# The next pair's high halves and query diagonal made a third of a step earlier, and its row maxima with them

## The chip, the cores and the metric

One core of one Trainium2 chip runs the kernel. The metric is device time in microseconds (us) of one execution; lower is better. A profiled execution has a span, from the first instruction of the program to the last, and its own device time, which is a little longer.

## What is computed

```python
def _attn_ref(q, k, v):                      # 4 batches, 8 heads, 1152 positions, 64 per head
    q_pool = q.reshape(B, H, S // 2, 2, D).mean(axis=3)
    scores = scale * np.matmul(q_pool, k.transpose(0, 1, 3, 2))
    scores = scores - np.max(scores, axis=-1, keepdims=True)
    attn = np.exp(scores)
    attn = attn / (np.sum(attn, axis=-1, keepdims=True) + 1e-09)
    return np.matmul(attn, v)
...
x = attn_out as 2304 tokens of 512
x = (silu(x @ w_gate) * (x @ w_val)) @ w_out          # inner width 1536
logits = x @ phi                                      # soft mixture, 8 experts x 4 slots
slot_input = softmax(logits over tokens).T @ x
slot_out[e] = relu(slot_input[e] @ w1[e]) @ w2[e]
return softmax(logits over slots) @ slot_out
```

Queries are pooled in twos, so a head has 576 query rows against 1152 keys. Scores are worked out in the precision of float32: each operand is split into a 16-bit high half and a 16-bit low half, and the products of the halves are summed.

## The kernel before

The sixteen pairs of heads (4 batches, 4 pairs each) are worked off in sixteen steps; `steps[i]` is pair i, and step i is the attention of pair i. Step i consists of 21 units of scores (`unit`): two matmuls each (L447 and L448) into a bank of PSUM, an exponential on ScalarE (L453, tile P) that takes the row maximum off by way of a row of QH, a subtraction on GpSimd that makes the low half of the result (L460, tile PL), and three units later the products with the values (L483 to L493, tile pv). `attn` yields 42 times in a step, twice a unit; f is the share of them that is past.

Before pair i can be worked off, its operands must be made (`split_pair`) and its row maxima must be known (`row_max`).

- `load_pair` brings keys, queries and values (kr, qr, vr) from memory; the buffers for kr and qr exist once.
- `split_pair(steps[i + 1])` runs at the start of step i (step 0: after 5 yields). It adds the two pooled queries in place (L257, VectorE), casts the keys' high half kh and the queries' high half qh (ScalarE, `cast`, L211), takes the low halves ql (L271, VectorE) and kl (L273, GpSimd), copies qh into the diagonal QD (two copies, L278, VectorE), starts twelve DMAs on SyncE's queue that lay the halves out per head in KK, QQ, KL and QH, and splits the values. kh, qh and QD exist once.
- QD holds head 0's queries in the upper 64 partitions and head 1's in the lower 64, with zeros elsewhere, so that one matmul against kh gives scores of both heads.
- `row_max` works the maxima from high halves alone: 18 matmuls of 512 columns and 9 of 128 (L366, tile mx, two banks), 21 reductions on VectorE (L372, L381, tile mp), one last reduction (L384, tile nm); two yields later ScalarE scales it (L352, tile mt) and starts a DMA from its own queue (L390) that writes the row of QH. The pair stands in `has_max` from then on. L448 is the matmul that reads this row.
- `maxima(n)` advances a single stream of all pairs' maxima to its n-th piece: 21 pieces for pair 0, 22 for each later pair. In step i (from 1 on) the main loop advances the pieces of pair i + 1 evenly between two shares of the step, `MX_BEG` and `MX_END`. In step 0 two other constants do it for pair 1.

From step 2 to step 8 the weights of the second stage are converted beside the attention (tiles r, lo, wgv, w2p); from step 4 on, matmuls of the second stage (L724 to L729, tiles g and v) fill in, paced by the steps (`MOE_PACE`): one block of 256 tokens until step 8 and 5.1 more until the end of step 15. The rest of the second stage and the mixture follow.

The order of each engine's instructions is laid down when the program is built, by a planner with a modelled timeline; what is written first goes first where both are ready, units of scores and the end of an accumulation are lifted by 20 places, and `after` and `not_before` set single orders by hand (a cast of the keys behind the mt DMA of the maxima before, the QD copies behind the nm before them). Each engine then works strictly in that order.

Of the kernel before, what the change touches and what calls it, by code (L numbers as in the profile page):

```python
# [10 lines left out]
F16 = mybir.dt.float16  # L11
# [26 lines left out]
ST_STEPS, ST_OF = 1, 3  # L38
HP_U0, HP_U1 = 20, 20
MX0, MXP = 21, 22  # L40
MX_BEG, MX_END = 0.05, 0.72
MX0_END, MX1_BEG, MX1_END = 0.34, 0.34, 0.84
PREP_LEAD = 3
HP_F = 20
# [33 lines left out]
def tile_pool_attention_glu_softmoe(  # L78
# [13 lines left out]
    nc = tc.nc  # L92
    B, NP, _, S = kT.shape
    SQ = qT.shape[4]
    D = 64
    P = 128
    NCH = S // P
# [4 lines left out]
    E, _, FE = w1.shape  # L102
# [24 lines left out]
    def after(ins, name):  # L127
        dep = mybir.DependencyInfo(mybir.DependencyClass.NoSync, mybir.DependencyReason.SCHED_ONLY)
        tc.add_manual_dep(ins.ins, name, dep, reason="pace")

    def not_before(ins, lead):

        if len(marks) > lead >= 0:
            after(ins, marks[-1 - lead])
# [31 lines left out]
    at = attn_stack.enter_context(tc.tile_pool(name="attn", bufs=1, side="right"))  # L166
# [14 lines left out]
    steps = [(b, p) for b in range(B) for p in range(NP)]  # L181
    raw = {}
    last_max = [None]
    QHs = {}
    st = {}

    NKQ = 2
    KLs = [at.tile([D + 1, 2, S], F16, name=f"KL{i}") for i in range(NKQ)]
    for t in KLs:
        nc.vector.memset(t[D:D + 1, :, :], 16.0)  # L190

    QD = at.tile([P, 2, SQ], F16, name="QD")
# [15 lines left out]
    def cast(what, b, p, dst, src):  # L208

        if b * NP + p < CAST_STEPS and what in CASTS:  # L210
            ins = nc.scalar.copy(dst, src)  # L211
        else:
            ins = nc.vector.tensor_copy(out=dst, in_=src)
        if p == 1 and b == 0 and what in "kvq":
            not_before(ins, 0)
        return ins

    def sub(what, b, p):

        i = b * NP + p  # L220
        return nc.gpsimd if i < len(SUBS) and what in SUBS[i] else nc.vector
# [6 lines left out]

    def first_split(kd, qd, KK, KL, QQ, QH):

        q = qd[:, :SQ]
        nc.vector.tensor_tensor(out=q, in0=q, in1=qd[:, SQ:], op=ALU.add)
        nc.vector.tensor_copy(out=QQ[:D, :], in_=q)
        nc.vector.tensor_copy(out=KK[:D, :], in_=kd)
        nc.scalar.copy(KK[D:, :], kd)
        nc.scalar.copy(QH[:D, :], QQ[:D, :])
        nc.gpsimd.tensor_tensor(out=QQ[D:, :], in0=q, in1=QQ[:D, :], op=ALU.subtract)
        nc.gpsimd.tensor_tensor(out=KL[:D, :], in0=kd, in1=KK[:D, :], op=ALU.subtract)

    def split_pair(b, p, first=None):  # L240
        kr, qr, vr = raw.pop((b, p))
        i = (b * NP + p) % NKQ
        KL = KLs[i]
        VV = at.tile([P, 2, NCH, 2, D + 1], F16, tag="VV", bufs=2, name=f"VV{b}_{p}")
        KK = at.tile([P, 2, S], F16, tag="KK", bufs=2, name=f"KK{b}_{p}")
        QQ = at.tile([P, 2, SQ], F16, tag="QQ", bufs=2, name=f"QQ{b}_{p}")
        QH = at.tile([D + 1, 2, SQ], F16, tag="QH", bufs=2, name=f"QH{b}_{p}")
        QHs[b, p] = QH
        for hd in range(2):
            st[b, p, hd] = (KK[:, hd, :], KL[:, hd, :], QQ[:, hd, :], QH[:, hd, :], VV[:, hd], vr[:, hd])  # L250
        if first:
            first_split(*first, KK[:, 0, :], KL[:, 0, :], QQ[:, 0, :], QH[:, 0, :])
            maxima(9)

        r = slice(D if first else 0, P)
        qp = qr[r, 0, :]
        add = sub("a", b, p).tensor_tensor(out=qp, in0=qp, in1=qr[r, 1, :], op=ALU.add)  # L257

        if (b, p) == steps[1]:
            after(add, last_max[0])  # L260
        elif not first:
            not_before(add, ADD_LEAD)
        kh = at.tile([P, S], F16, tag="kh", bufs=1, name=f"kh{b}_{p}")
        KHs[b, p] = kh
        k_cast = cast("k", b, p, kh[r], kr[r])
        if mt_name:
            after(k_cast, mt_name[-1])
        qh = at.tile([P, SQ], F16, tag="qh", bufs=1, name=f"qh{b}_{p}")
        q_cast = cast("q", b, p, qh[r], qp).ins.name
        ql = at.tile([P, SQ], F16, tag="ql", bufs=1, name=f"ql{b}_{p}")  # L270
        q_low = sub("l", b, p).tensor_tensor(out=ql[r], in0=qp, in1=qh[r], op=ALU.subtract).ins.name  # L271
        kl = at.tile([P, S], F16, tag="kl", bufs=1, name=f"kl{b}_{p}")
        k_low = nc.gpsimd.tensor_tensor(out=kl[r], in0=kr[r], in1=kh[r], op=ALU.subtract)  # L273
        rows = [slice(0, D), slice(D, P)]
        heads = range(1 if first else 0, 2)
        if not first:
            for hd in heads:
                ins = nc.vector.tensor_copy(out=QD[rows[hd], hd, :], in_=qh[rows[hd], :])  # L278
                if nm_name:
                    after(ins, nm_name[-1])  # L280
        for hd in heads:
            nc.sync.dma_start(out=KK[:D, hd, :], in_=kh[rows[hd], :])
            nc.sync.dma_start(out=KK[D:, hd, :], in_=kh[rows[hd], :])
        for hd in heads:
            nc.sync.dma_start(out=QQ[:D, hd, :], in_=qh[rows[hd], :])
            nc.sync.dma_start(out=QQ[D:, hd, :], in_=ql[rows[hd], :])
        for hd in heads:
            nc.sync.dma_start(out=KL[:D, hd, :], in_=kl[rows[hd], :])
            nc.sync.dma_start(out=QH[:D, hd, :], in_=qh[rows[hd], :])
        v_cast = cast("v", b, p, VV[:, :, :, 0, :], vr)  # L290
        if first:
            after(k_low, q_low)
            after(v_cast, q_cast)
        nc.gpsimd.tensor_tensor(out=VV[:, :, :, 1, :D], in0=vr[:, :, :, :D], in1=VV[:, :, :, 0, :D], op=ALU.subtract)  # L294
    def row_max_first(hd):
# [59 lines left out]
    mt_name, nm_name = [], []  # L355
    has_max = {steps[0]}
# [43 lines left out]
    def later(n, fn):  # L400

        due.append((now[0] + n, fn))
# [18 lines left out]
    def maxima(n):  # L421
        while n_rm[0] < min(n, MX0 + MXP * (len(steps) - 1)):
            next(maxs)
            n_rm[0] += 1
# [38 lines left out]
    def pv_rem(acc, PH, PL, b, p, parts):  # L463

        for i in range(0, len(parts), 2):
            c = parts[i][1]
            todo = []
            for z in range(2):
                dst = acc[z * D:(z + 1) * D, 4, :]
                VV, vr = st[b, p, z][4:]  # L470
                q = slice((i + z) * REM, (i + z + 1) * REM)
                if PL is None:
                    todo.append([(dst, PH[:, q], vr[:, c, :])])
                else:
                    todo.append([
                        (dst[:, :D + 1], PH[:, q], VV[:, c, 0, :]),
                        (dst[:, :D], PH[:, q], VV[:, c, 1, :D]),
                        (dst[:, :D + 1], PL[:, q], VV[:, c, 0, :]),
# [501 lines left out]
    first = first_load()  # L980
# [52 lines left out]
    def moe_due(t):  # L1033
        for (t0, m0), (t1, m1) in zip(MOE_PACE, MOE_PACE[1:]):
            if t < t1:
                return QPB * (m0 + (m1 - m0) * (t - t0) / (t1 - t0))
        return QPB * MOE_PACE[-1][1]

    n_done = 0
    for i, (b, p) in enumerate(steps):  # L1040
        for u, _ in enumerate(attn(b, p)):
            if i == 0 and u == PHI_U:
                nc.sync.dma_start(out=ph, in_=phi.rearrange("p (d s) -> p d s", d=ND))
            tick()
            f = (u + 1) / UNITS
            if u == (SPLIT0 if i == 0 else 0):
                if i + 1 < len(steps):
                    split_pair(*steps[i + 1])
                if i + 2 < len(steps):
                    later(0 if i == 0 else LOAD_LAG, lambda k=i + 2: load_pair(*steps[k]))  # L1050

            if i:
                maxima(MX0 + MXP * i + int(MXP * min(1.0, max(0.0, f - MX_BEG) / (MX_END - MX_BEG))))
            else:
                maxima(9 + int((MX0 - 9) * min(1.0, f / MX0_END)) + int(MXP * min(1.0, max(0.0, f - MX1_BEG) / (MX1_END - MX1_BEG))))
            while i >= MOE_START and n_done < moe_due(i + f):
                if not next(moe_work, False):
                    break
                n_done += 1
            while prep and n_prep - len(prep) < (i + f - PREP_BEG) * n_prep / (PREP_END - PREP_BEG):  # L1060
                prep.pop(0)()
            if not prep and u == LOAD_U and LOAD_STEP <= i < LOAD_STEP + NEE:
                load(i - LOAD_STEP, marks[-1])
# [28 lines left out]
    for z in range(2):  # L1092
        (nc.vector.tensor_copy, nc.scalar.copy)[z](
            out=GT.rearrange("p (f h c) s -> p f h c s", h=2, c=2)[:, :, z],
            in_=t.rearrange("p (f c) h s -> p f c h s", c=2)[:, :, :, z],
# [51 lines left out]
    for e in range(4):  # L1147
        r = slice(e * NS, e * NS + E // 4 * SPE)
# [6 lines left out]
    for g in range(E // NQ):  # L1155
        for h in range(2):
# [13 lines left out]
            for e in range(NQ):  # L1170
                a = NQ * g + e
                nc.vector.tensor_copy(
                    out=hT[:, NQ * h:NQ * (h + 1), a, g, :],
                    in_=t[:, :, e * NS + SPE * a:e * NS + SPE * (a + 1)],
# [112 lines left out]
```

## Time and profile before

| | |
|---|---|
| median of 3 runs | 879.44 us (874.75, 879.44, 883.06) |
| the profiled execution's own time | 874.95 us |
| its span | 873.2 us |
| mean granted TensorE clock | 0.979 |
| busy: TensorE matmuls, weight loads | 817.1 us (94%), 579.0 us (66%) |
| busy: VectorE, ScalarE, GpSimd | 540.4 us (62%), 393.3 us (45%), 414.4 us (47%) |

PE is TensorE, PEld its weight loads, DVE VectorE, ACT ScalarE, POOL GpSimd, SP SyncE; a q behind a name is the engine's sequencer, which issues DMAs. Matmuls overlap in the array and their ends are modelled, so a stretch in which PE is called busy isn't always one in which it could take no more. The rows of a timeline give start, duration, engine, line and tiles, and in brackets how long the engine had been idle before and what ended that. The rows of windows give a stretch, its length, the busy time (and count) of PE, PEld, DVE, ACT and POOL, the granted clock as a share of 2.4 GHz, the DMA share and GB/s.

### The profile page before, as it was taken

What the parts mean: (1) busy time and instruction counts of PE and PEld (TensorE: products, weight loads), DVE (VectorE), ACT (ScalarE), POOL (GpSimd) and SP (SyncE); (2) the same over time, 40 slices, a digit from 0 to 9 for tenths busy, and PEclk for the clock granted to TensorE, in tenths of its full rate; (3) what the DMA queues carried; (4) which work ended last, traced back from release to release, by engine and by line L of the source; (5) the groups of instructions that cost most, each with busy time, mean ns of one, the idle gap of its engine ahead of it and who ended that gap; (6) DMA issues with size and microseconds to landing.
All of it is one profiled execution on the core that took longest, in us unless ns stands there. A gap on an engine that the chain in (4) does not pass through costs nothing.

```text
span 873.2 us, 23665 instructions
## 1 busy us (share of the span) xinstructions
PE 817.1 (94%) x9952; PEld 579.0 (66%) x9952; DVE 540.4 (62%) x1060; ACT 393.3 (45%) x739; POOL 414.4 (47%) x380
## 2 busy tenths in 40 slices
PE   5978988999799899999999999999999999998896
PEld 2545656776576667777777777777777777776345
DVE  7957868588777767566666666576734344445223
ACT  4545868676677743435343444335334312112112
POOL 7978666454558654646565555546445200000100
PEclk9989989999899999999999999999999999999998
DMA  6563766859577551527343453413112399358999
GB/s 196 144 157 95 228 162 229 263 135 266 137 202 194 170 135 33 135 59 141 113 108 80 127 135 102 106 31 74 26 38 38 90 304 308 61 155 222 295 284 290
DMA packets 151868, 132.48 MB, mean 152 GB/s; under 512 B 83152, under 2 KB 120720, under 8 KB 151760
## 3 DMA queue, kind: packets, MB, share of 16 engines
q1 hardware_dynamic: 149600, 130.92, 56.2%
q8 instruction: 78, 1.28, 0.6%
q10 hardware_dynamic: 2160, 0.04, 0.1%
q14 instruction: 30, 0.25, 0.1%
HBM read 84.10 MB, written 7.86 MB: 105 GB/s over the span
## 4 chain that ended last, share of the span: by engine, by line
PE 75%; DVE 12%; DMA 5%; ACT 3%; issue 2%; SPq 1%; POOL 1%; ACTq 0%; DVEq 0%
PE st L448 7%; PE st L447 7%; PE mx L366 6%; PE g L724 5%; PE g L729 5%; PE g L728 5%; PE v L724 5%; PE v L729 5%; PE v L728 5%; DVE mp L372 3%; PE pv L491 3%; PE pv L492 3%; PE pv L493 3%; PE pv L483 2%; PE hp L1160 2%
## 5 line engine op out<-in xcount | busy, mean ns | idle before, releaser
L460 POOL TENSOR_TENSOR PL<-P 128x512 f16<-128x512 f32 (+1 forms) x311 | 326.2, 1061 | 238.0 <-ACT P L453 232.0
L453 ACT ACTIVATE P<-st 128x512 f32<-128x512 f32 (+1 forms) x336 | 191.2, 582 | 215.8 <-PE st L448 182.0
L372 DVE TENSOR_REDUCE mp<-mx 128x1 f32<-128x512 f32 x270 | 180.1, 686 | 68.8 <-PE mx L366 66.2
L448 PE MATMUL st<-QH,KL 65*128 65x512 f16 (+1 forms) x576 | 145.9, 294 | 8.1 <-DMA QH<-mt 5.5
L447 PE MATMUL st<-QQ,KK 128*128 128x512 f16 (+1 forms) x576 | 146.0, 292 | 3.8 <-ACT P L453 3.6
L492 PE MATMUL pv<-VV,P 128*128 128x64 f16 x1088 | 139.8, 196 | 0.3 <-POOL VV L294 0.3
L491 PE MATMUL pv<-VV,P 128*128 128x65 f16 x1088 | 138.6, 194 | 0.9 <-DVE x L523 0.8
L493 PE MATMUL pv<-VV,PL 128*128 128x65 f16 x1088 | 135.9, 193 | 0.2 <-POOL PL L460 0.2
L724 PE MATMUL g<-xT,wgv 128*128 128x256 f16 x432 | 119.2, 276 | 3.9 <-DVE hs L736 2.7
L729 PE MATMUL g<-xT,wgv 128*128 128x256 f16 x432 | 119.1, 276 | 1.4 <-DVE wgv L689 1.4
L728 PE MATMUL g<-xT,wgv 128*128 128x256 f16 x432 | 119.0, 275 | 0.0
L491 PEld LDWEIGHTS <-P 128*128 128x128 bf16 x1088 | 104.2, 98 | 21.7 <-issue 4.1
L724 PE MATMUL v<-xT,wgv 128*128 128x256 f16 x432 | 117.9, 273 | 0.5 <-DVE wgv L689 0.5
L729 PE MATMUL v<-xT,wgv 128*128 128x256 f16 x432 | 117.9, 273 | 0.0
L728 PE MATMUL v<-xT,wgv 128*128 128x256 f16 x432 | 117.9, 273 | 0.0
L366 PE MATMUL mx<-kh,QD 128*128 128x512 f16 x270 | 105.1, 407 | 12.6 <-DVE QD L278 6.0
L493 PEld LDWEIGHTS <-PL 128*128 128x128 f16 x1088 | 104.1, 100 | 10.7 <-POOL PL L460 2.1
L492 PEld LDWEIGHTS <-P 128*128 128x128 bf16 x1088 | 103.6, 98 | 10.7 <-issue 2.3
L728 PEld LDWEIGHTS <-wgv 128*128 128x128 f16 x864 | 84.9, 98 | 21.3 <-issue 6.2
L724 PEld LDWEIGHTS <-wgv 128*128 128x128 f16 x864 | 85.3, 99 | 19.5 <-issue 3.5
L729 PEld LDWEIGHTS <-wgv 128*128 128x128 f16 x864 | 84.8, 98 | 17.6 <-DVE wgv L689 1.5
L448 PEld LDWEIGHTS <-KL 65*128 65x128 f16 x576 | 51.8, 98 | 33.5 <-issue 13.3
(184 smaller groups left out, 1190.8 us busy)
## 6 DMA issues: line engine op xcount, KB each, us to landing
w<-in_w SPq DMA_DIRECT2D x16, 1024.0 KB, 7.4
w<-in_w SPq DMA_DIRECT2D x64, 256.0 KB, 5.4
vr<-in_vP SPq DMA_DIRECT2D x16, 585.0 KB, 5.8
KK<-kh SPq DMA_DIRECT2D x62, 144.0 KB, 3.6
qr<-in_qT SPq DMA_DIRECT2D x15, 576.0 KB, 4.5
kr<-in_kT SPq DMA_DIRECT2D x15, 576.0 KB, 4.8
r<-in_w_out SPq DMA_DIRECT2D x12, 512.0 KB, 4.4
r<-in_w_gate SPq DMA_DIRECT2D x24, 256.0 KB, 5.9
```

The lines of the kernel that those rows point to most:

```text
L366: nc.tensor.matmul(t, q, kh[:, k0:k0 + kw], start=True, stop=True)
L372: nc.vector.reduce_max(out=mp[:, g, c:c + 1], in_=t, axis=AX.X)
L447: nc.tensor.matmul(t[:, o:o + w], KK[:, k], QQ[:, q0:q0 + w], start=True, stop=False)
L448: nc.tensor.matmul(t[:, o:o + w], KL[:, k], QH[:, q0:q0 + w], start=False, stop=True)
L453: marks.append(nc.scalar.activation(P32[:, :o], t[:, :o], AF.Exp, scale=1.0 / 16.0).ins.name)
L460: eng.tensor_tensor(out=PL[:, :o], in0=P32[:, :o], in1=PH[:, :o], op=ALU.subtract)
L491: nc.tensor.matmul(dst[:, :D + 1], PH[:, q], VV[:, c, 0, :], start=first, stop=False, skip_group_check=True)
L492: nc.tensor.matmul(dst[:, :D], PH[:, q], VV[:, c, 1, :D], start=False, stop=False, skip_group_check=True)
L493: nc.tensor.matmul(dst[:, :D + 1], PL[:, q], VV[:, c, 0, :], start=False, stop=(c == NCH - 1), skip_group_check=True)
L724: mm = nc.tensor.matmul(o, w[:, 0, d, f], xh, start=(d == 0), stop=False)
L728: nc.tensor.matmul(o, w[:, 0, d, f], xl, start=False, stop=False)
L729: nc.tensor.matmul(o, w[:, 1, d, f], xh, start=False, stop=(d == ND - 1))
```

## The change

The pooled add, both casts to high halves and the two QD copies leave `split_pair` for a function of their own, `split_high`. For a pair k of 2 or later it is called as soon as the maxima of pair k - 1 are complete (`has_max`) and pair k has been loaded, which is in step k - 2; `split_pair(k)` at the start of step k - 1 makes the rest as before. The maxima of pair k run from 0.9 of step k - 2 to 0.6 of step k - 1, where they ran from 0.05 to 0.72 of step k - 1. Pairs 0 and 1 keep their places. Nothing is computed more or less.

```diff
-MX_BEG, MX_END = 0.05, 0.72
+MX_BEG, MX_END = -0.1, 0.6
...
+    highs = {}
+
+    def split_high(b, p, first=None):
+        kr, qr, _ = raw[b, p]
...
+        add = sub("a", b, p).tensor_tensor(out=qp, in0=qp, in1=qr[r, 1, :], op=ALU.add)
...
+        kh = at.tile([P, S], F16, tag="kh", bufs=1, name=f"kh{b}_{p}")
+        KHs[b, p] = kh
+        k_cast = cast("k", b, p, kh[r], kr[r])
+        if mt_name:
+            after(k_cast, mt_name[-1])
+        qh = at.tile([P, SQ], F16, tag="qh", bufs=1, name=f"qh{b}_{p}")
+        q_cast = cast("q", b, p, qh[r], qp).ins.name
+        rows = [slice(0, D), slice(D, P)]
+        for hd in range(0 if first else 2):
+            ins = nc.vector.tensor_copy(out=QD[rows[hd], hd, :], in_=qh[rows[hd], :])
+            if nm_name:
+                after(ins, nm_name[-1])
+        highs[b, p] = r, qp, kh, qh, q_cast
+
     def split_pair(b, p, first=None):
-        kr, qr, vr = raw.pop((b, p))
+        if not first and (b, p) not in highs:
+            split_high(b, p)
+        kr, qr, vr = raw[b, p]
...
+        if first:
+            split_high(b, p, first)
+        del raw[b, p]
+        r, qp, kh, qh, q_cast = highs.pop((b, p))
...
-            if i:
-                maxima(MX0 + MXP * i + int(MXP * min(1.0, max(0.0, f - MX_BEG) / (MX_END - MX_BEG))))
-            else:
+            if i == 0:
                 maxima(9 + int((MX0 - 9) * min(1.0, f / MX0_END)) + int(MXP * min(1.0, max(0.0, f - MX1_BEG) / (MX1_END - MX1_BEG))))
+            for k in (i + 1, i + 2):
+                if 2 <= k < len(steps):
+                    if steps[k - 1] in has_max and steps[k] in raw and steps[k] not in highs:
+                        split_high(*steps[k])
+                    if steps[k] in highs or steps[k] in QHs:
+                        part = (i + f - (k - 1) - MX_BEG) / (MX_END - MX_BEG)
+                        maxima(MX0 + MXP * (k - 1) + int(MXP * min(1.0, max(0.0, part))))
```

## Rows read from the trace of the kernel before

**Rows 1.** The page's head and busy time of the engines.
```profile
span 873.2 us, 23665 instructions
...
PE 817.1 (94%) x9952; PEld 579.0 (66%) x9952; DVE 540.4 (62%) x1060; ACT 393.3 (45%) x739; POOL 414.4 (47%) x380
```
**Rows 2.** Windows: steps 1 to 7, then steps 8 to 14.
```profile
43.70:296.90 253.20, 227.35 (x3005) 157.49 (x3005) 189.47 (x351) 170.90 (x325) 163.57 (x140) 0.95 0.68 189
296.90:646.00 349.10, 345.37 (x4284) 253.00 (x4284) 226.18 (x434) 146.56 (x274) 188.88 (x163) 1.00 0.40 93
```
**Rows 3.** Waits of PE from 40 to 300 us: total, times, longest.
```profile
PE mx L366 <- DVE QD L278: 6.0, 2, 3.2
PE st L448 <- DMA QH<-mt: 5.5, 3, 3.8
...
PE st L448 <- DMA KK<-kh: 2.6, 1, 2.6
PE mx L366 <- ACT kh L211: 2.2, 1, 2.2
```
**Rows 4.** Timeline of PE where one pair hands over to the next.
```profile
77.71 0.38 PE L448 MATMUL st<-QH,KL 65*128 65x512 f16 x1 [0.79 <-DMA QH<-mt]
...
82.48 1.06 PE L366 MATMUL mx<-kh,QD 128*128 128x512 f16 x2 [3.22 <-DVE QD L278]
...
114.30 1.07 PE L366 MATMUL mx<-kh,QD 128*128 128x512 f16 x2 [2.75 <-DVE QD L278]
...
230.10 1.01 PE L448 MATMUL st<-QH,KL 65*128 65x512 f16 x2 [3.85 <-DMA QH<-mt]
```
**Rows 5.** Windows: stretches at half clock behind those places; the sum takes all four.
```profile
82.50:85.90 3.40, 3.40 (x20) 1.68 (x21) 1.93 (x3) 0.60 (x1) 1.82 (x2) 0.50 0.47 126
113.20:120.00 6.80, 5.70 (x42) 2.72 (x43) 4.61 (x7) 1.94 (x4) 3.55 (x4) 0.50 0.74 199
...
sum 20.40, PE 18.14 PEld 9.39 DVE 11.51 ACT 5.45 POOL 11.17; mean PE 4.53 PEld 2.35 DVE 2.88 ACT 1.36 POOL 2.79
```
**Rows 6.** Timelines of DVE, ACT and POOL from 72.5 to 83 us.
```profile
73.89 0.18 DVE L384 TENSOR_REDUCE nm<-mp 128x9 f32<-128x27 f32 x1
...
79.11 3.31 DVE L278 COPY QD<-qh 64x576 f16<-64x576 f16 x2
...
76.02 1.14 ACT L211 CAST kh<-kr 128x1152 f16<-128x1152 f32 x1
77.06 0.67 ACT L211 CAST qh<-qr 128x576 f16<-128x576 f32 x1
...
78.53 2.88 POOL L273 TENSOR_TENSOR kl<-kr,kh 128x1152 f16<-128x1152 f32 x1
```
**Rows 7.** Groups by line, 43.7 to 296.9 us: busy, mean ns, idle before.
```profile
L453 ACT ACTIVATE P<-st 128x512 f32<-128x512 f32 (+1 forms) x148 | 83.8, 583 | 43.8 <-PE st L448 26.3 <-PE pv L492 9.8 <-POOL PL L460 2.6
...
L278 DVE COPY QD<-qh 64x576 f16<-64x576 f16 x14 | 12.0, 860 | 0.1
...
L211 ACT CAST kh<-kr 128x1152 f16<-128x1152 f32 x7 | 8.1, 1152 | 1.6 <-DMA QH<-qh 1.1 <-ACT mt L352 0.6
...
L211 ACT CAST qh<-qr 128x576 f16<-128x576 f32 x7 | 4.8, 680 | 0.0
```
**Rows 8.** All QD copies of the run: shortest, median, longest ns.
```profile
L278 DVE COPY QD<-qh x30: 289/694/2459, 24.9 to 594.2; 64x576 f16<-64x576 f16 x30
```
**Rows 9.** Waits of ACT from 43.7 to 296.9 us, and one mt issue.
```profile
ACT mt L352 <- DVE nm L384: 3.1, 1, 3.1
...
225.18 0.48 ACTq L390 DMA_DIRECT2D QH<-mt  x1
```
**Rows 10.** Chain that ended last: the load of kr for pair 5, and mt.
```profile
128.28 0.58 SPq L201
...
144.93 3.14 DMA QH<-mt
```
**Rows 11.** DMA issues of the page: count, KB, median us to landing.
```profile
kr<-in_kT SPq DMA_DIRECT2D x15, 576.0 KB, 4.8
```

More of the change, by code (lines that the diff above doesn't have):

```diff
@@ L238, in first_split @@
         nc.gpsimd.tensor_tensor(out=KL[:D, :], in0=kd, in1=KK[:D, :], op=ALU.subtract)
-    def split_pair(b, p, first=None):
-        kr, qr, vr = raw.pop((b, p))
[L242 to L253, printed above, removed]
+    highs = {}
+    def split_high(b, p, first=None):
+        kr, qr, _ = raw[b, p]
         r = slice(D if first else 0, P)
@@ L269, in split_pair @@
         q_cast = cast("q", b, p, qh[r], qp).ins.name
+        rows = [slice(0, D), slice(D, P)]
[4 more added lines that the diff above has]
+        highs[b, p] = r, qp, kh, qh, q_cast
+    def split_pair(b, p, first=None):
+        if not first and (b, p) not in highs:
+            split_high(b, p)
+        kr, qr, vr = raw[b, p]
+        i = (b * NP + p) % NKQ
+        KL = KLs[i]
+        VV = at.tile([P, 2, NCH, 2, D + 1], F16, tag="VV", bufs=2, name=f"VV{b}_{p}")
+        KK = at.tile([P, 2, S], F16, tag="KK", bufs=2, name=f"KK{b}_{p}")
+        QQ = at.tile([P, 2, SQ], F16, tag="QQ", bufs=2, name=f"QQ{b}_{p}")
+        QH = at.tile([D + 1, 2, SQ], F16, tag="QH", bufs=2, name=f"QH{b}_{p}")
+        QHs[b, p] = QH
+        for hd in range(2):
+            st[b, p, hd] = (KK[:, hd, :], KL[:, hd, :], QQ[:, hd, :], QH[:, hd, :], VV[:, hd], vr[:, hd])
+        if first:
+            first_split(*first, KK[:, 0, :], KL[:, 0, :], QQ[:, 0, :], QH[:, 0, :])
+            maxima(9)
+        if first:
+            split_high(b, p, first)
+        del raw[b, p]
+        r, qp, kh, qh, q_cast = highs.pop((b, p))
         ql = at.tile([P, SQ], F16, tag="ql", bufs=1, name=f"ql{b}_{p}")
@@ L275, in split_pair @@
         heads = range(1 if first else 0, 2)
[L276 to L280, printed above, removed]
         for hd in heads:
```

## The prediction

> **What bounds the kernel now.** I read the page's head first: the matmuls are called busy for 817.1 of 873.2 us [rows 1], so TensorE sets the time and a change like this one, which computes nothing less, can win only time in which TensorE stands idle or runs slowly. Then windows, to see where that is. I cut the run at the first score matmul of pair 1 and of pair 8. In steps 1 to 7 TensorE is busy 227.35 of 253.2 us, which leaves 25.9 us idle, 36.2 us a step; in steps 8 to 14 it is busy 345.37 of 349.1 us, which leaves 3.7 us [rows 2]. The late steps are filled by the second stage's matmuls; whatever the change does for order there is worth next to nothing. So the case is decided in the early steps, where no other engine is full either: VectorE 189.47, ScalarE 170.9 and GpSimd 163.57 of 253.2 us [rows 2].
>
> Third, the waits of TensorE there. The long ones all hang on the two things that the change moves: 6.0 us for the diagonal QD, 5.5 us for the row of QH that the maxima's DMA brings, and 2.6 and 2.2 us in the hand-over from step 0 to step 1 [rows 3]. The timeline shows them at the hand-overs: 0.79 and 3.22 us where pair 2 begins, 2.75 us where pair 3 begins, 3.85 us where pair 6 begins [rows 4]; the third wait for QH is what is left of the 5.5, 0.9 us. Fourth, the clock. Behind these places stand stretches with a granted clock of 0.50, the 1.2 GHz level, 20.4 us in the sum, with TensorE busy for 18.14 us of it [rows 5]; before each of them it had stood idle for one of these waits. A matmul at half clock takes twice its time, so 18.14 / 2 = 9.1 us of them are the clock's.
>
> **The maxima end earlier.** The maxima of pair k are due when step k begins. In the program they ended at 0.72 of the step before, in the trace much later: the mt DMA of pair 6 was issued at 225.18, and the first matmul that needs it ran at 230.10 after waiting 3.85 us [rows 4, 9]. The change ends them 0.12 of a step earlier, 0.12 x 36.2 = 4.3 us. That is more than the longest of the three latenesses (3.85), so I book the whole 5.5 us as gone. What comes next there is the exponential of the same unit, which follows the scores in any case.
>
> **The diagonal is made earlier.** In the hand-over to step 2 the chain from the last reduction to the end of the copies runs from 73.89 (nm) over the casts at 76.02 and 77.06 to the copies at 79.11 that take 3.31 us, so to 82.42: 8.5 us [rows 6]. The old program left 0.05 of a step for it, 1.8 us. The new one starts it at about 0.65 of a step (0.6, and two of 42 yields until the pair stands in has_max) and needs it at 0.9: 0.25 x 36.2 = 9.1 us. That just covers 8.5 us, and the two copies should be shorter there: at 79.11 they stood beside kl, a 2.88 us subtraction on GpSimd [rows 6], and kl stays at the start of the step. So I book the 6.0 us for QD as gone too. Direct gain: 6.0 + 5.5 = 11.5 us.
>
> **The clock.** If the waits go, the four half-clock stretches should go. Bounds: 0, if TensorE only waits for other engines there instead, and 9.1 us, if it is the limit throughout. In the first stretch TensorE is busy without a break (3.40 of 3.40), in the second it has idle time even at half clock (5.70 of 6.80) [rows 5]. That lies between the ends, and I take half, 4.5 us.
>
> **What the moved instructions cost.** ScalarE has both casts in mid-step now, 1.15 + 0.68 = 1.83 us a pair [rows 7], among exponentials that flow, where they had stood in a hand-over in which ScalarE waited for scores anyway. There are 148 exponentials in 253.2 us, one per 1.71 us, of which one takes 0.58 [rows 7]: 1.13 us spare. So 1.83 - 1.13 = 0.70 us a pair may come through to TensorE, which waits for the score bank; times 7 pairs, 4.9 us. Bounds: 0 (two score banks hold it) and 7 x 1.83 = 12.8 us. I take 4.9, as rows 7 are of the same stretch. The pooled add and the QD copies (860 ns each [rows 7]) go to a third of the step in which VectorE has no maxima to reduce: nothing, with 253.2 - 189.47 = 63.7 us of VectorE idle as cover; without it they cost what they take beyond now, below.
>
> The twelve DMAs of `split_pair`, ql, kl and the values' split keep their place, so SyncE's queue is passed by nothing. But the casts now need the loads about a third of a step sooner, and a cast that waits for kr would hold all exponentials behind it on ScalarE. The tightest early one I see: kr of pair 5 was issued at 128.28, and with 4.8 us to landing it is there at 133.1; the cast stands behind the mt of pair 4, whose DMA was issued at 144.93 and would come some 4.3 us sooner, at 140.6 [rows 10, 11]. That leaves 7.5 us. I book nothing.
>
> The hand-over from step 0 to 1 (2.6 + 2.2 us [rows 3]) I leave as it is: the cast of pair 2 stands behind the mt of pair 1 in both programs, and pair 1's maxima keep their constants. Bounds: 4.8 us either way.
>
> **Sum.** 11.5 + 4.5 - 4.9 = 11.1 us. Against the profiled execution: 874.95 - 11.1 = 863.9. That execution is as fast as the fastest of the three timed runs, 4.5 us under their median, so the median of the changed kernel should be 879.44 - 11.1 = 868.3 us. One per cent of it, 8.8 us, is about what can be told from no change: the three runs before spread over 8.3 us. The threshold for faster is 870.6 us.
>
> **Rival 1: the maxima don't end earlier on the chip.** They already run behind the program: nm of pair 2 came at 73.89 [rows 6], 30.2 us after step 1 began at 43.7, where 0.72 of a mean step is 26.1 us. Units of scores are lifted ahead of them, and the planner may let them lag more. Then the waits for QH stay, with the half clock behind them. What is left is the QD waits, 6.0, and half of the clock loss behind those two, (3.40 + 5.70) / 2 / 2 = 2.3 [rows 5], less 4.9: 3.4 us, so 876 us. For it speaks the lag itself; against it, that VectorE, which limits the pieces' pace, has a quarter of its time free [rows 2]. Chance 0.18.
>
> **Rival 2: the copies get slower in mid-step.** The QD copies take from 289 to 2459 ns [rows 8], and the two that stood beside kl took 3.31 us together [rows 6]. GpSimd works on PL through most of a step. At 2.46 us each instead of 0.86, seven pairs cost 7 x 2 x 1.6 = 22.4 us of VectorE's time; if half of it delays the maxima, which wait behind the copies, 11.2 us eat the gain: 879 us. Against it: the copies' median of 694 ns over the whole run [rows 8], where GpSimd works as well. Chance 0.10. [...]
>
> **Rival 3, slower: ScalarE is held in mid-step.** ScalarE works strictly in order, and the new program has mt, its DMA issue and both casts in a row in the middle of flowing exponentials. mt waits for nm; the one such wait here is 3.1 us, and the issue takes 0.48 [rows 9]. With the casts ScalarE would be held for 3.1 + 0.48 + 1.83 = 5.4 us. Two score banks cover 2 x 1.71 = 3.4 us; 2.0 us come through, in 14 steps 28 us. Less the gain of 16.0 that still comes (11.5 + 4.5), 12 us slower: 891 us. It decides from a hold over 3.4 us, so only if nm is late in most steps; it was so once in seven pairs [rows 9]. Chance 0.13.
>
> **How the numbers follow.** The forecast has 0.59; its own range is 859 (all of the clock loss and casts at nothing: 11.5 + 9.1 = 20.6 us) to 875 (clock at nothing and casts at some 7 us: 4.5 us). About 0.50 of its 0.59 lie under 870.6. Faster by over 1%: 0.50. Slower by over 1%: 0.13, rival 3. Within: 0.37. The range should reach 855 below (the 20.6 us and some of the spread of the runs) and 886 above, over rivals 1 and 2 and the edge of rival 3.
>
> **What would show it.** Right: L366 waits for QD and L448 for the mt DMA no more in steps 2 to 7; the QD copies of pair k begin at 0.65 to 0.75 of step k - 2; mt of pair k is issued some 4 us before step k begins; no stretch of half clock at the hand-overs after the first; steps 1 to 7 take about 242 us instead of 253.2 and steps 8 to 14 the same 349. Wrong: waits of L447 for the exponentials grow by more than 5 us (casts in the way), mt is still issued as the pair begins (rival 1), the copies stand at 2 us and more (rival 2), or L201's landings appear as what ScalarE waits for.

## The result, and the profile after

The changed kernel takes 865.74 us, the median of 4 runs (864.63 to 867.71); beside it the kernel before took 881.25 us (874.75 to 887.87). The ratio is 0.9848, with a 95% interval of 0.9804 to 0.9892: some 13 us faster. Forecast were 868, from 855 to 886.

The windows of the changed kernel answer to [rows 2]; cut at the same places, the first score matmuls of pairs 1, 8 and 15 (columns as there):

```profile
47.70:288.60 240.90, 222.34 (x3014) 156.65 (x3013) 196.46 (x356) 171.28 (x329) 164.92 (x141) 0.99 0.73 201
288.60:634.80 346.20, 344.62 (x4270) 252.25 (x4269) 219.66 (x428) 144.28 (x270) 186.83 (x162) 1.00 0.41 92
```

Steps 1 to 7 went from 253.2 to 240.9 us, steps 8 to 14 from 349.1 to 346.2. In steps 1 to 7 TensorE's idle time fell from 25.9 to 18.6 us, its busy time from 227.35 to 222.34 us, and the mean granted clock rose from 0.95 to 0.99. The waits of TensorE there, of the changed kernel from 40 to 292 us, answer to [rows 3]:

```profile
PE pv L505 <- DVE x L537: 4.8, 4, 2.2
PE st L461 <- ACT P L467: 4.3, 9, 1.0
PE mx L380 <- DVE mp L386: 2.9, 8, 0.7
PE st L462 <- DMA QH<-mt: 2.7, 3, 1.8
PE mx L380 <- ACT kh L211: 1.4, 2, 1.2
...
```

No matmul waits for QD any more, and the wait for the row of QH is halved. The longest that is left of it, 1.8 us, belongs to pair 1, whose place the change leaves alone, and 0.46 us lie in step 8; in steps 2 to 7 it is 0.44 us. One wait grew: value matmuls wait 4.8 us for VectorE (L537, which empties the accumulator), 0.8 us before. L460 of before is L474 here, L447 and L448 are L461 and L462, L366 is L380, L372 is L386, L384 is L398.

Where in steps 1 to 7 the time went is told by windows of single steps. First the kernel before, steps 1 to 6:

```profile
43.70:76.20 32.50, 26.85 (x377) 17.52 (x377) 21.08 (x41) 15.70 (x30) 25.84 (x23) 0.89 0.48 122
76.20:115.40 39.20, 31.37 (x432) 21.47 (x432) 30.88 (x51) 27.44 (x53) 28.83 (x24) 0.93 0.70 192
115.40:145.70 30.30, 29.52 (x405) 20.46 (x402) 22.47 (x45) 21.76 (x43) 18.01 (x16) 0.92 0.69 201
145.70:188.60 42.90, 39.84 (x453) 29.73 (x447) 30.61 (x56) 28.76 (x53) 22.05 (x18) 0.96 0.63 187
188.60:221.00 32.40, 31.22 (x440) 21.15 (x436) 25.93 (x48) 22.46 (x44) 17.66 (x16) 1.00 0.87 245
221.00:262.40 41.40, 36.04 (x469) 25.04 (x466) 30.66 (x60) 28.14 (x54) 24.34 (x23) 0.92 0.68 178
```

Then the same steps of the changed kernel:

```profile
47.70:83.90 36.20, 29.64 (x395) 19.26 (x394) 28.70 (x49) 17.29 (x31) 30.14 (x26) 0.91 0.49 126
83.90:117.00 33.10, 28.30 (x405) 19.79 (x402) 25.45 (x48) 24.87 (x49) 22.20 (x19) 1.00 0.66 196
117.00:148.20 31.20, 28.77 (x392) 20.11 (x391) 25.36 (x45) 23.72 (x47) 22.08 (x19) 1.00 0.83 235
148.20:185.70 37.50, 36.73 (x464) 28.04 (x460) 26.64 (x51) 26.79 (x53) 20.38 (x19) 1.00 0.76 209
185.70:219.30 33.60, 33.46 (x473) 24.30 (x470) 30.28 (x57) 25.37 (x49) 18.75 (x17) 1.00 0.89 238
219.30:253.50 34.20, 32.62 (x451) 22.62 (x449) 29.49 (x55) 25.83 (x53) 24.49 (x21) 1.00 0.75 213
```

Steps 2, 4 and 6 lost 6.1, 5.4 and 7.2 us, 18.7 together. They are the steps that held the waits of [rows 4]: both QD waits and one QH wait lie in step 2, the QH waits of pairs 4 and 6 in steps 4 and 6. Steps 1, 3, 5 and 7 gave 6.4 us back (3.7 of it in step 1): 18.7 - 6.4 = 12.3 us, the whole difference of the stretch. But a step doesn't hold the same work in both kernels: step 1 has 18 more matmuls than before, step 2 27 fewer, step 5 33 more, so part of what one step lost has only moved into its neighbour. Steps taken in twos tell more: 1 and 2 went from 71.7 to 69.3 us, 3 and 4 from 73.2 to 68.7, 5 and 6 from 73.8 to 67.8, and step 7 from 34.5 to 35.1. The first two, with 6.8 us of waits for QD and QH before, gained 2.4 us; the other four, with 4.7 us of them, gained 10.5.

The chain of pair 3 in the changed kernel, on VectorE, answers to [rows 6]:

```profile
74.02 0.18 DVE L398 TENSOR_REDUCE nm<-mp 128x9 f32<-128x27 f32 x1
74.11 1.33 DVE L263 COPY QD<-qh 64x576 f16<-64x576 f16 x2
```

The two copies take 1.33 us where they took 3.31, and are ready 8.5 us before step 2 begins. The cast of qh had already run at 69.23, ahead of nm, and that of kh follows at 75.55 and takes 1.15 us, so from nm to the last of them it is 2.7 us, where the prediction had read 8.5 from the kernel before. Over the run they are shorter too; this row of all QD copies answers to [rows 8]:

```profile
L263 DVE COPY QD<-qh x30: 291/308/2325, 26.8 to 574.7; 64x576 f16<-64x576 f16 x30
```

And the hand-over to pair 6, where the longest QH wait had been:

```profile
217.76 0.48 ACTq L404 DMA_DIRECT2D QH<-mt  x1
...
220.74 0.60 PE L462 MATMUL st<-QH,KL 65*128 65x512 f16 x2 [0.44 <-DMA QH<-mt]
```

3.85 us of waiting have become 0.44. The mt DMA is issued 1.5 us before step 6 begins; before, it was issued 4.2 us after [rows 9].

### The profile page after: what moved, and what is told of

The parts are those of the page before. It is cut to its first block, busy times and chain, and to the rows that moved or that the text cites. A ratio compares the mean times of both kernels' runs of the same rounds, so it can differ in the third digit from the quotient of the medians.

```text
span 863.9 us, 23702 instructions
## 1 busy us (share of the span) xinstructions
PE 816.8 (95%) x9952; PEld 580.0 (67%) x9952; DVE 541.2 (63%) x1060; ACT 392.5 (45%) x739; POOL 414.0 (48%) x380
## 4 chain that ended last, share of the span: by engine, by line
PE 75%; DVE 12%; DMA 7%; ACT 3%; issue 2%; SPq 0%; ACTq 0%; DVEq 0%
PE st L462 7%; PE st L461 7%; PE mx L380 6%; PE g L738 5%; PE g L743 5%; PE g L742 5%; PE v L738 5%; PE v L743 5%; PE v L742 5%; DVE mp L386 3%; PE pv L497 3%; PE pv L505 3%; PE pv L506 3%; PE pv L507 3%; PE hp L1179 2%
## 5 line engine op out<-in xcount | busy, mean ns | idle before, releaser
L474 POOL TENSOR_TENSOR PL<-P 128x512 f16<-128x512 f32 (+1 forms) x311 | 326.0, 1061 | 230.0 <-ACT P L467 227.7
L386 DVE TENSOR_REDUCE mp<-mx 128x1 f32<-128x512 f32 x270 | 179.9, 684 | 55.9 <-PE mx L380 53.0
L461 PE MATMUL st<-QQ,KK 128*128 128x512 f16 (+1 forms) x576 | 143.7, 291 | 5.1 <-ACT P L467 4.3
L462 PE MATMUL st<-QH,KL 65*128 65x512 f16 (+1 forms) x576 | 144.4, 293 | 2.7 <-DMA QH<-mt 2.7
L505 PE MATMUL pv<-VV,P 128*128 128x65 f16 x1088 | 136.8, 193 | 4.9 <-DVE x L537 4.8
L506 PE MATMUL pv<-VV,P 128*128 128x64 f16 x1088 | 136.7, 195 | 0.0
L506 PEld LDWEIGHTS <-P 128*128 128x128 bf16 x1088 | 103.2, 98 | 10.4 <-issue 2.2
L380 PE MATMUL mx<-kh,QD 128*128 128x512 f16 x270 | 103.8, 402 | 6.6 <-DVE mp L386 3.1
L738 PEld LDWEIGHTS <-wgv 128*128 128x128 f16 x864 | 85.1, 98 | 18.6 <-issue 2.1
L462 PEld LDWEIGHTS <-KL 65*128 65x128 f16 x576 | 51.7, 99 | 33.0 <-issue 14.9
## 6 DMA issues: line engine op xcount, KB each, us to landing
w<-in_w SPq DMA_DIRECT2D x64, 256.0 KB, 5.5
r<-in_w_gate SPq DMA_DIRECT2D x24, 256.0 KB, 5.1
```

The source lines that it names most:

```text
L380: nc.tensor.matmul(t, q, kh[:, k0:k0 + kw], start=True, stop=True)
L386: nc.vector.reduce_max(out=mp[:, g, c:c + 1], in_=t, axis=AX.X)
L461: nc.tensor.matmul(t[:, o:o + w], KK[:, k], QQ[:, q0:q0 + w], start=True, stop=False)
L462: nc.tensor.matmul(t[:, o:o + w], KL[:, k], QH[:, q0:q0 + w], start=False, stop=True)
L474: eng.tensor_tensor(out=PL[:, :o], in0=P32[:, :o], in1=PH[:, :o], op=ALU.subtract)
L505: nc.tensor.matmul(dst[:, :D + 1], PH[:, q], VV[:, c, 0, :], start=first, stop=False, skip_group_check=True)
```

## The experiments

Ratios are to the kernel before, run on the same chip, with 95% intervals; times of steps come from windows cut as above.

**The kernel before, once more** (no edit).

> The unchanged kernel once more, for a second trace. The four timed runs of it spread from 874.75 to 887.87 us, those of the changed kernel from 864.63 to 867.71 us. If the hand-overs are what varies (theory: waits for QD and for the row of QH, and the half clock behind them), a run of 880 us or more shows more than 11.5 us of these two waits or more than 20.4 us of half clock behind them. Rival: the extra time lies in the last 230 us, where the weights of the experts are loaded, and the hand-overs are as before within 2 us.

It took 880.97 us, with a span of 879.1 us against 873.2. Steps 1 to 7, and the last stretch from the second stage's end:

```profile
46.20:299.50 253.30, 228.00 (x3006) 156.95 (x3005) 190.08 (x351) 170.95 (x325) 163.71 (x140) 0.95 0.67 189
...
812.70:879.10 66.40, 59.49 (x658) 32.29 (x658) 15.74 (x59) 11.74 (x23) 0.88 (x4) 0.89 0.98 278
```

The rival was right in the main: steps 1 to 7 are the same to 0.1 us, TensorE waits 6.0 us for QD in both and 4.7 instead of 5.5 us for the row of QH, and the 5.9 us lie mostly in step 0 (46.2 us against 43.7) and in the last stretch, 66.4 us here, with a clock of 0.89, and 63.1 us in the first trace, with 0.96; in between, steps 8 to 14 took 1.7 us less and the stretch behind them 1.7 us more. The execution that the prediction rests on was a short one in its first and last stretch. The two first profiles differ by 9.3 us and the medians by 15.5; against this second trace the changed kernel's span is 15.2 us shorter, 3.8 us of that in the last stretch (62.6 us), which the change doesn't touch. Single steps differ too between these two executions, by up to 1.9 us (step 6: 41.4 and 39.5).

**The early high halves alone**, an edit of the changed kernel, and **the early end alone**, an edit of the kernel before.

```diff
-MX_BEG, MX_END = -0.1, 0.6
+MX_BEG, MX_END = 0.05, 0.72
```

> The high halves and the diagonal made early, the maxima at 0.05 to 0.72 as in the kernel before. Theory (both parts count): the QD waits of 6.0 us go with half clock worth some 4.5 us behind them, the QH waits stay, so 6 to 10 us faster than before, ratio 0.988 to 0.993. Rival (the earlier end does it all): no faster than 2 us. Rival (the early diagonal does it all): 12 to 16 us faster, as the whole change.

```diff
-MX_BEG, MX_END = 0.05, 0.72
+MX_BEG, MX_END = 0.05, 0.6
```

> The kernel before with the maxima from 0.05 to 0.6 instead of 0.72; the high halves stay where they were. Theory: the QH waits of 5.5 us go with half clock worth some 4.5 us, the QD waits stay, so 6 to 10 us faster, ratio 0.988 to 0.993. Rival (VectorE, which must reduce 22 pieces in 0.55 of a step instead of 0.67, or the QD chain at the step's start holds them back): the maxima end as late as before and it is no faster than 2 us.

Neither wins anything. The early high halves alone: 879.85 us, ratio 0.9977 (0.9927 to 1.0027). The early end alone: 881.65 us, 1.0033 (0.9997 to 1.0069). Both of my expectations of 6 to 10 us fell. The waits of TensorE with the high halves alone (40 to 303 us), and windows of its steps 1, 2, 4 and 6:

```profile
PE st L461 <- ACT P L467: 7.1, 12, 1.5
PE pv L505 <- DVE x L537: 5.3, 3, 2.5
PE st L462 <- DMA KK<-kh: 4.3, 1, 4.3
...
PE st L462 <- DMA QH<-mt: 0.8, 1, 0.8
```
```profile
46.50:85.40 38.90, 29.62 (x391) 19.09 (x389) 24.90 (x46) 16.99 (x31) 27.91 (x24) 0.87 0.42 117
85.40:119.10 33.70, 28.65 (x420) 19.88 (x417) 24.49 (x47) 25.09 (x49) 22.66 (x21) 1.00 0.65 193
...
150.20:194.90 44.70, 42.54 (x459) 31.30 (x458) 28.72 (x54) 28.63 (x55) 21.00 (x17) 0.89 0.62 175
...
228.20:268.80 40.60, 35.56 (x485) 24.88 (x484) 33.33 (x63) 29.63 (x56) 26.31 (x22) 0.96 0.62 176
```

The QD waits are gone and step 2 has its gain (33.7 us, 39.2 before). But step 1 takes 38.9 us instead of 32.5, and steps 4 and 6 are as long as before. The waits for the row of QH are nearly gone as well, 0.8 us of 5.5. So this kernel has lost 10.7 of the 11.5 us of waits that the prediction booked, and its steps 1 to 7 take 256.0 us instead of 253.2: other waits grew (for exponentials 7.1 us, 3.1 before; for VectorE's L537 5.3, 0.8 before; for KK 4.3, 2.6 before). Step 4 has a clock of 0.89: behind a wait of 1.54 us for an exponential, at 160.09, TensorE stands at half clock from 162 to 172 us. With the early end alone step 6 has its gain and step 4 hasn't; in its waits from 40 to 300 us TensorE waits 10.5 us for the high halves where it was 8.2 before, and 3.1 us of that for kh in step 4:

```profile
PE mx L366 <- DVE QD L278: 5.3, 2, 3.2
PE mx L366 <- ACT kh L211: 5.2, 2, 3.1
```
```profile
149.80:194.60 44.80, 40.14 (x451) 29.45 (x451) 31.45 (x59) 30.62 (x57) 21.04 (x17) 0.92 0.64 178
...
229.80:264.90 35.10, 32.20 (x453) 22.55 (x452) 27.37 (x52) 25.75 (x49) 23.96 (x21) 0.95 0.75 204
```

**The early beginning with the late end**, an edit of the changed kernel.

```diff
-MX_BEG, MX_END = -0.1, 0.6
+MX_BEG, MX_END = -0.1, 0.72
```

> The changed kernel with the maxima from -0.1 to 0.72 instead of 0.6: early high halves and an early beginning, the late end of before. Theory: the QH waits come back in part, 3 to 7 us slower than the changed kernel (869 to 873 us on the scale of its 865.7). Rival (the end of the window doesn't matter, since the planner sets the order): within 2 us of the changed kernel.

884.2 us, ratio 1.0049 (1.0014 to 1.0084): neither expectation held, it is a little slower than the kernel before. The end of the window matters much more than I had thought, 0.12 of a step for 2% of the kernel. In these kernels it also sets when the high halves of the next pair are made, since `split_high` waits for `has_max`; the edit moves both. From here the theory was one of two gates: the maxima can end early only if QD is there and if the window lets them.

**Both gates, without the early beginning**, an edit of the changed kernel, run twice.

```diff
-MX_BEG, MX_END = -0.1, 0.6
+MX_BEG, MX_END = 0.05, 0.6
```

> Early high halves with the maxima from 0.05 to 0.6: the changed kernel without its early beginning. So far neither the early high halves alone (ratio 0.998), nor the early end alone (1.003), nor both early high halves and early beginning with the late end (1.005) won anything. New theory (two gates in a row: the maxima can end early only if the diagonal is there in time and if the window lets them): this one has both gates open and wins most of it, ratio 0.984 to 0.990. Rival (the beginning ahead of the step is the third gate, since a pair's pieces take over 20 us whatever the window says): 0.993 or more.

> Early high halves with the window of 0.05 to 0.6 once more, for a closer interval: it had ratio 0.9816 (0.9762 to 0.9871), the changed kernel 0.9848 (0.9804 to 0.9892). Theory (the early beginning adds nothing): 0.980 to 0.986. Rival (its good value was chance): 0.987 or more.

863.43 us, ratio 0.9816 (0.9762 to 0.9871), and again 865.84 us, 0.9813 (0.9781 to 0.9845). That is the whole gain, and more than my first range had for it: the part of the change that lets the maxima begin at 0.9 of the step before adds nothing that can be told. Its interval overlaps that of the changed kernel, so it isn't shown to be the better version either.

**Other ends**, two edits of the changed kernel, with a beginning at 0.05.

```diff
-MX_BEG, MX_END = -0.1, 0.6
+MX_BEG, MX_END = 0.05, 0.66
...
+MX_BEG, MX_END = 0.05, 0.54
```

> Early high halves, window of 0.05 to 0.66. Theory (the end of the window opens the gate by degrees between 0.72, ratio 0.998, and 0.60, 0.982): about half, 0.986 to 0.994. Rival (no gate: what differs between these kernels is which small wait happens to fall where in the planner's order, and whether the clock drops behind it): anything from 0.980 to 1.005 with no order in the ends, and the time of steps 1 to 7 goes with the time at half clock in them, not with how late the row of QH lands.

> Early high halves, window of 0.05 to 0.54. Theory (gates): open, so as at 0.60, ratio 0.979 to 0.987. Rival (small waits and the clock behind them): anything from 0.980 to 1.005, again with the time at half clock: under 10 us of it in steps 1 to 7 if these take under 245 us, over 15 us if they take over 250.

| end of the window | ratio (95% interval) | step 4 | step 6 | steps 1 to 7 | mean clock in them |
|---|---|---|---|---|---|
| 0.72 | 0.9977 (0.9927 to 1.0027) | 44.7 us | 40.6 us | 256.0 us | 0.95 |
| 0.66 | 0.9921 (0.9889 to 0.9953) | 42.0 us | 40.3 us | 244.6 us | 0.97 |
| 0.60 (second time) | 0.9813 (0.9781 to 0.9845) | 37.2 us | 35.6 us | 241.3 us | 0.97 |
| 0.54 | 0.9848 (0.9799 to 0.9897) | 35.8 us | 33.3 us | 242.5 us | 0.96 |

Windows of steps 4 and 6, first with the end at 0.66, then at 0.54:

```profile
144.30:186.30 42.00, 38.63 (x473) 28.88 (x470) 28.78 (x54) 28.48 (x55) 20.88 (x18) 1.00 0.64 190
...
219.10:259.40 40.30, 36.06 (x477) 25.44 (x475) 31.50 (x62) 29.11 (x55) 27.01 (x22) 0.92 0.61 178
```
```profile
149.50:185.30 35.80, 35.53 (x443) 27.03 (x442) 24.07 (x47) 25.90 (x51) 20.39 (x17) 1.00 0.72 200
...
220.00:253.30 33.30, 31.96 (x464) 22.78 (x463) 28.74 (x54) 26.94 (x52) 25.48 (x22) 1.00 0.78 219
```

The order is the one that the gate theory asks for: nearly half of the gain at 0.66, all of it at 0.60, no more at 0.54, and steps 4 and 6 shrink in that order too. The traces show the gates themselves. The mt DMA of pair 4 is issued 2.7, 4.1, 5.9 and 8.4 us before step 4, in the order of the table, and that of pair 6 5.2 and 2.8 us after the start of step 6, then 0.5 and 0.6 us before it; in the kernel before it is 0.8 us before and 4.2 after, with the early end alone 1.8 and 1.3 us after. What the earlier row pays by isn't shown. It isn't TensorE's waiting for it: these waits are 0.8, 1.6, 3.2 and 2.1 us from 40 to some 300 us, in the order of the table. And the end moves the high halves with it: pair 6's QD copies start at 0.89 of step 4 with 0.72, at 0.77 with 0.60.

The rival, that these kernels differ by chance in the planner's order and by the clock that drops behind small waits, would have given no order. One of its marks fails: at 0.54 the mean clock of 0.96 means some 2 x 0.04 x 242.5 = 19 us at half clock (an estimate: fifteen windows of the kernel before, cut around its stretches at half clock, show 1.00 or 0.50 and nothing between), and yet the steps take under 245 us. But an order of four is no proof, and the next kernel falls out of it.

**Earlier still**, an edit of the changed kernel.

```diff
-MX_BEG, MX_END = -0.1, 0.6
+MX_BEG, MX_END = -0.2, 0.5
```

> The changed kernel with the maxima from -0.2 to 0.5. In the changed kernel the row of QH still lands after the first score matmul of pairs 6, 7 and 8 (by 1.4, 4.8 and 0.8 us). Theory (the lateness of that row is what costs): these go, 0 to 4 us faster than the changed kernel. Rival (what is left is VectorE and ScalarE between the hand-overs, and the maxima now press on the end of the step before): same within 1 us or 2 to 6 us slower, with longer waits of the value matmuls for VectorE's L537.

881.63 us, ratio 1.0023 (0.9986 to 1.006). The gain is lost: by the ratios some 15 us slower than the changed kernel, more than the rival's 2 to 6, and not where either looked. The row did come earlier, as the theory wanted: the mt DMAs of pairs 4 and 6 are issued 9.2 and 6.8 us before their steps, and steps 6 and 7 take 69.8 us, 69.3 in the changed kernel. So both gates open are not enough. Waits from 146 to 190 us, and the window of step 4:

```profile
PE w2p L680 <- ACT r L674: 2.7, 1, 2.7
...
ACT VV L211 <- DMA vr<-in_vP: 2.2, 1, 2.2
```
```profile
146.50:190.20 43.70, 41.04 (x453) 30.98 (x450) 30.38 (x54) 28.04 (x54) 19.77 (x18) 0.88 0.59 157
```

In step 4 ScalarE holds the cast of a pair's values until their load has landed, 2.2 us; a copy that TensorE needs (L674) stands behind it, and TensorE waits 2.7 us. Step 4 takes 43.7 us at a mean clock of 0.88, step 5 42.1 us. This is the kind of wait that I had looked for and not found with the loads of the keys. Behind that wait it stands at half clock from 158 to 168 us. One trace shows it; that it makes the whole difference of steps 4 and 5 isn't shown.

**The cast twice**, an edit of the changed kernel.

```diff
         k_cast = cast("k", b, p, kh[r], kr[r])
+        if not first and (b, p) != steps[1]:
+            k_cast = cast("k", b, p, kh[r], kr[r])
```

> The changed kernel with the cast of the keys' high half made twice on ScalarE for pairs 2 to 15, 1.15 us more a pair in mid-step. Prediction's term (a cast comes through to TensorE for what exceeds 1.13 us of slack; two casts are already over it): the whole 1.15 us in each of seven early pairs, 8 us, and up to 16 us in all fourteen. Rival (the score banks hide the casts and the term of 4.9 us was none): 2 us or less slower.

876.97 us, ratio 0.9958 (0.9925 to 0.9991), against 0.9848 for the changed kernel. Its steps 1 to 7, then its steps 5 and 6:

```profile
46.90:295.50 248.60, 223.72 (x3014) 157.34 (x3013) 191.27 (x355) 178.38 (x337) 165.33 (x141) 0.99 0.70 195
...
184.30:223.90 39.60, 36.48 (x479) 25.98 (x476) 34.81 (x65) 29.44 (x55) 20.94 (x18) 1.00 0.76 204
223.90:260.90 37.00, 34.26 (x478) 23.26 (x474) 26.67 (x51) 26.66 (x52) 24.68 (x23) 1.00 0.71 197
```

248.6 - 240.9 = 7.7 us, and seven casts of 1.15 us are 8.1 us. The sum fits the theory, but the place doesn't: steps 5 and 6 take 6.0 and 2.8 us more than in the changed kernel, the other five together 1.1 us less. So it isn't shown that each cast comes through. The edit also leaves only the second of the two casts tied behind the mt DMA, so the planner may lay out another order. Steps 8 to 14 take 346.4 us, 0.2 more; there TensorE doesn't notice it.

**The late pairs alone**, an edit of the changed kernel.

```diff
+LATE = 9
...
-                    if steps[k - 1] in has_max and steps[k] in raw and steps[k] not in highs:
+                    if k >= LATE and steps[k - 1] in has_max and steps[k] in raw and steps[k] not in highs:
...
+                        beg, end = (MX_BEG, MX_END) if k >= LATE else (0.05, 0.72)
-                        part = (i + f - (k - 1) - MX_BEG) / (MX_END - MX_BEG)
+                        part = (i + f - (k - 1) - beg) / (end - beg)
```

> The change for pairs 9 to 15 alone; pairs 2 to 8 keep the split at the start of the step and the window of 0.05 to 0.72. Theory (only the steps before 8 have time to win): within 3 us of the kernel before, ratio 0.996 to 1.000. Rival (the gain is spread over all steps, or comes from the order of the last ones): half of it or more, ratio under 0.993.

875.91 us, ratio 0.9966 (0.9929 to 1.0003): some 3 us of the 13, and by the interval 6 at the most, come from the late pairs, in line with the windows of steps 8 to 14 (349.1 and 347.4 us in the two traces of the kernel before, 346.2 in the changed kernel).

**The clock**, an edit of the kernel before, in `row_max` and in `unit`; the filling computes nothing that is kept.

```diff
+    def fill(t, n):
+        for _ in range(n):
+            nc.tensor.matmul(t[:, :P], id16, id16, start=True, stop=True)
...
+                if 2 <= b * NP + p <= 8 and g == 0 and c == 0:
+                    fill(t, 24)
...
+        if 2 <= b * NP + p <= 8 and key < 2:
+            fill(t, 12)
```

> The kernel before with filling matmuls for pairs 2 to 8: twelve of 128 columns into the bank of scores ahead of each of a pair's first two units, and twenty-four into the first bank of its maxima, 48 a pair, whose results are overwritten; at 53 ns (128 columns at 2.4 GHz, from matmuls of 512 columns that start 0.21 us apart) 2.6 us a pair, 18 us in all. Theory (the clock at the hand-overs costs 9 us, and idle time of 11.5 us there takes some of the filling in): half clock behind the hand-overs falls from over 20 us to under 10, and steps 1 to 7 take 245 to 257 us instead of 253, far from 18 us more. Rival (the clock costs nothing, since other engines limit there, or it does not follow such filling): half clock stays over 15 us, or steps 1 to 7 take 262 us or more.

896.39 us, ratio 1.0182 (1.0145 to 1.0219). Its steps 1 to 7:

```profile
46.90:315.50 268.60, 247.63 (x3326) 178.15 (x3325) 193.55 (x353) 173.17 (x328) 164.38 (x140) 0.97 0.64 178
```

The clock rose from 0.95 to 0.97, and the stretch still grew by 15.4 us for some 18 us of filling (an estimate: 336 matmuls of 128 columns, each a quarter of the 0.21 to 0.22 us between the starts of two of 512). This filling pays nothing, as the rival said. What half clock costs the kernel it can't tell. What it costs a matmul is in the trace of the kernel before, first at a clock of 0.50, then at 1.00:

```profile
83.34 0.63 PE L447 MATMUL st<-QQ,KK 128*128 128x512 f16 x1
83.77 0.63 PE L448 MATMUL st<-QH,KL 65*128 65x512 f16 x1
...
89.55 0.38 PE L447 MATMUL st<-QQ,KK 128*128 128x512 f16 x1
89.76 0.38 PE L448 MATMUL st<-QH,KL 65*128 65x512 f16 x1
89.98 0.38 PE L366 MATMUL mx<-kh,QD 128*128 128x512 f16 x1
```

From one start to the next it is 0.43 us for 512 columns at 0.50, and 0.21 to 0.22 us at 1.00: twice the time. That is some 1.2 and 2.4 columns a ns, and so, with a column counted as a cycle, the 1.2 and 2.4 GHz named above (an estimate). By the mean clocks of steps 2, 3, 4 and 6 the time at half clock behind these hand-overs fell from some 20 to some 7 us (an estimate, 2 x (1 - clock) x length). But the filling stands ahead of the scores, and TensorE's waits for exponentials (40 to 310 us) went from 3.1 us to:

```profile
PE st L455 <- ACT P L461: 10.4, 13, 2.2
```

Two executions of one program tell more. These are the kernel with the window of 0.05 to 0.6, the first and the second time: steps 1 to 7, then step 1, step 6 and the last stretch:

```profile
47.30:288.30 241.00, 219.56 (x3012) 156.02 (x3011) 194.76 (x351) 170.79 (x327) 165.48 (x142) 0.99 0.72 201
...
47.30:82.00 34.70, 28.18 (x395) 18.37 (x394) 27.82 (x49) 17.28 (x30) 29.92 (x26) 0.95 0.51 131
218.80:253.30 34.50, 30.94 (x470) 22.24 (x467) 28.13 (x51) 25.44 (x49) 24.83 (x21) 1.00 0.75 209
797.50:860.10 62.60, 54.99 (x658) 28.93 (x658) 15.75 (x59) 11.74 (x23) 0.92 (x4) 0.96 1.04 295
```
```profile
44.20:285.50 241.30, 221.32 (x3010) 156.75 (x3009) 193.96 (x350) 170.68 (x328) 165.84 (x142) 0.97 0.72 200
...
44.20:80.00 35.80, 29.26 (x395) 18.60 (x394) 28.10 (x49) 17.29 (x31) 30.04 (x26) 0.90 0.49 127
215.60:251.20 35.60, 32.45 (x470) 23.19 (x468) 28.35 (x53) 25.47 (x49) 24.57 (x22) 0.95 0.72 202
795.10:861.60 66.50, 59.60 (x658) 32.52 (x658) 15.79 (x59) 11.75 (x23) 0.84 (x4) 0.89 0.97 277
```

Over the whole stretch two hundredths of the clock go with only 0.3 us. But the clock differs in steps 1 and 6 alone, and each of these took 1.1 us more the second time, for some 3.5 us more at half clock (2 x 0.05 x 35, an estimate); the other five steps have the same clock and took 0.1 to 0.7 us less. In the last stretch, at 0.89 instead of 0.96, TensorE was busy 4.6 us longer and the stretch took 3.9 us more. So a lower clock goes with lost time here, some third of the time at half clock in the two steps; with single steps that vary by up to 1.9 us, that is a hint and no measurement.

## Why the prediction was right, and which of its steps were not

The place and the size were right: 11.1 us were booked, steps 1 to 7 were to take 242 us and take 240.9, steps 8 to 14 were to stay and lost 2.9. The ratio's interval is 9.5 to 17.3 us of 881.25, and 11.1 lies in it. But the sum was right for reasons that in part don't hold, so its closeness is partly luck.

- The waits went as booked: of the QD waits (6.0 us) nothing is left, of the QH waits (5.5 us) 0.44 in steps 2 to 7. The step that fails is to book a wait of TensorE that goes as time won, and the two as a sum of separate gains. The early high halves alone took away 10.7 us of these waits and won nothing that can be told, since other waits grew in their place; the early end alone won nothing either, and both together 13 us. In the changed kernel steps 1 and 2, which had held 6.8 us of the waits, gained 2.4 us, and steps 3 to 6, which had held 4.7, gained 10.5. What the two parts win together is shown; by which mechanism stays open.
- Of the clock I took half of 9.1 us. That a matmul takes twice its time there is shown by its starts (0.43 us apart for 512 columns, against 0.21 to 0.22); what the kernel loses by it isn't: the runs neither refute the half nor measure it. TensorE's busy time in steps 1 to 7 fell by 5.0 us at nearly the same number of matmuls while the clock rose from 0.95 to 0.99, which agrees with the 4.5; one program at a lower clock took 1.1 us more in each of two steps; and filling, with which the clock rose from 0.95 to 0.97, paid nothing, and TensorE waited 10.4 us for exponentials, 3.1 before.
- The casts' term (4.9 us) isn't shown. Casting twice cost 7.7 us, near to the 8.1 of the casts, but in two steps and not in seven; waits of L461 for exponentials grew only from 3.1 to 4.3 us in the changed kernel. The 4.8 us of the value matmuls' waiting for VectorE is something the prediction didn't have.
- The earlier end: booked as 4.3 us. Against the starts of their steps the mt DMAs of pairs 2 to 8 are issued 3.8 us earlier on average, from 0.6 (pair 3) to 8.0 us (pair 2), and the hand-over to pair 6 kept 0.44 us of 3.85. The end of the window was the deciding number; 0.66 gives only some two fifths of the gain.
- The early beginning at 0.9, which the prediction used for the room of 9.1 us that the QD chain has, isn't needed: with a beginning at 0.05 the result is the same.
- Of the signs, the QD copies of pairs 3 to 6 begin at 0.61 to 0.77 of step k - 2 (pair 3 at 0.73: 74.11 between 47.7 and 83.9), about as said, but those of pairs 7 to 9 at 0.92 to 0.96. mt of pairs 2 to 5 is issued 6.6 to 9.4 us before the step, of pairs 6 and 8 1.5 and 2.1 us before, and of pair 7 1.1 us after its start.

Rival 1 (the maxima don't end earlier on the chip) is refuted by the times at which the mt DMAs are issued; what remains of it is that pairs 6 to 8 still have little room. Rival 2 (slower copies) is refuted: the copies' median fell from 694 to 308 ns. They still spread, from 291 to 2325 ns, but the longest is at pair 1, which keeps its place: its two copies take 3.72 us from 26.84, beside kl on GpSimd (2.37 us from 25.68). What makes a copy long isn't shown. Rival 3 (ScalarE held in mid-step) didn't come in the changed kernel, but the kernel with the window of -0.2 to 0.5 shows a case like it, with a load in the place of nm. There the order on ScalarE held: the copy L674, whose last input came from a matmul of 152.82 to 153.20, ran at 156.57, behind the cast that waited for its load until 155.48.

## What to carry to other kernels

Where two things must be early in each round of a pipeline, one edit that moves either may measure as nothing; try them together before dropping one, and then take the pieces away singly to see which are needed. A wait that is gone from the profile is not yet time won: here 10.7 of 11.5 us went and the kernel stayed as slow, as other waits grew. Read the gain by the round, but count first whether the rounds hold the same work; here matmuls had moved between them, and only steps taken in twos could be compared. An end point as 0.6 is to be tried on both sides: the gain came by degrees from 0.72 to 0.60, and a whole window set earlier lost it again, in its one trace beside a load that came too late for ScalarE.

## What the runs showed that I had not expected

- Filling matmuls, with which the clock rose from 0.95 to 0.97, won nothing: some 18 us of them (an estimate) cost 15.4 us in a stretch in which TensorE had been idle for 10% of the time.
- One program took 0.3 us more over steps 1 to 7 at a clock of 0.97 instead of 0.99, but 1.1 us more in each of the two steps whose clock was lower; only single steps show it.
- A wait of 2.2 us on ScalarE for a load of values came in a step that took 43.7 us instead of 37.5, at a clock of 0.88.
- Two executions of the kernel before differ by 5.9 us, nearly all of it in step 0 and in the last 66 us (2.5 and 3.3 us), and not in steps 1 to 7: 253.2 and 253.3 us.
